# A due-time plan for the attention part of a fused attention, Fourier-mixing and MLP kernel

## The chip, the cores and the metric

The kernel runs on one core of a Trainium2 chip. Its five engines work in parallel, each through its own queue in the queue's order: TensorE (PE) with its matmuls and, beside them, weight loads; VectorE (DVE); ScalarE (ACT); GpSimd (POOL); and SyncE (SP), which here issues DMAs. An instruction that waits for a semaphore holds up everything behind it on its engine. The metric is the device time of one execution in microseconds (us).

## The reference

Batch 8, 8 heads, 576 positions, 64 values a head, all in f32. Causal attention with a decay bias comes first; then a Fourier mixing over positions and channels, a layer norm and an MLP. Cut to what matters:

```python
cum = np.cumsum(np.maximum(s, 0), axis=-1)
bias = -(cum[:, :, :, None] - cum[:, :, None, :])
scores = where(causal, -1e9, scale * q @ k.T + minimum(bias, 0))
attn = exp(scores - max); attn /= attn.sum() + 1e-9
x = (attn @ v).transpose(0, 2, 1, 3).reshape(8, 576, 512)
u = x + real(fft(fft(x, axis=1), axis=2))
un = (u - mean) / sqrt(var + 1e-6)
out = u + relu(un @ w1) @ w2            # 512 -> 2048 -> 512
```

## The kernel before

**Attention.** The 64 heads are handled as `NP` = 32 pairs, four pairs a batch. A pair `i` goes through the same steps, each a generator that yields between its instructions. `load` brings `qk` (SP's DMA). `high` has ACT round `qk` into `KQ`, and a DMA puts the rows of cumulated decay into it from `cumD`. `low` has two DMAs bring the rounded halves across partitions to `Q` and `K`, DVE form the remainder `K`, POOL the remainder `Q`, and a DMA load `va`. `maxes` has, for each head, five blocks of queries: PE multiplies into a PSUM bank `pm`, DVE takes the maximum of each query into a column of `Mx`; then PE transposes `Mx` into `pmt`, ACT copies that to `mt`, and a DMA puts `mt` as one row into `KQ`, so that the score product subtracts the maximum by itself. `scores` has PE multiply twice into a bank `ps`, ACT take the exponential `P`, POOL zero the causal corner. `av` has PE multiply `P` with `va` into `pav` (two banks a head), ACT copy the result to `stage` and `rows`, and DMAs collect the sums of the exponentials. `recip` has DVE take their reciprocals, and DMAs spread them through DRAM (`rd`) to `rb`. `finish` has POOL multiply, and for two of the four pairs of a batch DMAs bring the product, reversed, to `xs`.

**Mixing.** When a batch has its four pairs, `folds` adds and subtracts `xa` and `xs` (`Aw` on DVE, `Bw` on POOL, `Df`, `De`, `Do`), and `fourier` multiplies them with the tables in two stages (`pzs`, `pzc`, then `pyc`, `pys`) and stores `uD`.

**Conversion.** `convert_w` turns twelve pieces of the MLP's weights into two words each, beside the attention, and stores them in `wD`.

**What sets the order.** For pairs 0 to 30 a loop builds, for each pair, a list of these generators with quotas (of the next pair's `maxes`, this pair's `scores`, the last pair's `av`, a share of the mixing and so on), and `weave` takes from each in turn by its share. There only PE's order is the written one, by

```python
order.enter_context(tc.manual_schedule(engines={mybir.EngineType.PE}))
```

and a scheduler puts the instructions of the other engines in their queues. For the last pair, and all that comes behind it (the last mixing, the layer norm and the MLP), the order is written out for all engines by a planner, `Flow`: each step is a generator that yields (engine, cost, what it depends on, ring of buffers) before each instruction and has a due time; the planner keeps a time at which each engine is free, and of the steps that can start next on an engine it places the one with the earliest due time:

```python
t, s = min(ready, key=lambda x: (x[1][3][0] is not None, x[0]))
engine = s[3][0]
t, s = min(((u, v) for u, v in ready if v[3][0] == engine and u <= t + 0.05), key=lambda x: x[1][1])
```

A due time sets an order only; on the chip an instruction starts when the one before it on its engine is through and its semaphores are there.

**Banks.** PSUM has three banks `ps` for scores and mixing (`bank`), and five banks under one tag `m` for `pm`, `pmt` and `pav`. The buffers `KQ`, `Q`, `K` are there three times, `P` four times, `xa` and `xs` twice.

**Behind the attention** the MLP takes two token tiles in a plain way and then seven in `fast_tile`, with PE's products `b`, `h` and `acc`.

## Time and profile before

| | us |
|---|---|
| three runs | 1404.06, 1411.13, 1412.85 |
| their median | 1411.13 |
| the profiled execution | 1416.26 |
| its span in the profile | 1414.6 |
| PE busy in it | 1280.3 (91%) |
| DVE busy | 817.8 (58%) |
| ACT busy | 634.4 (45%) |
| POOL busy | 517.0 (37%) |

The mean clock granted to PE over the span is 0.962 of full speed. A busy time adds up all instructions of an engine, over stages in which different things set the pace, so a share alone does not say what bounds the kernel. In the page's digit rows the span is cut in 40 slices of 35.4 us; a digit is the busy share in tenths. In a row of a window table the numbers are the engines' busy times in one stretch of the span, then the granted clock. In a timeline or a group, `[4.62 <-DMA xs<-xr]` says that the engine stood 4.62 us ahead of the instruction, and what ended that. `SPq` and `ACTq` are issues of DMAs on the queues of SP and ACT.

### The profile page before, as it was taken

What the parts mean: (1) busy time and instruction counts of PE and PEld (TensorE: products, weight loads), DVE (VectorE), ACT (ScalarE), POOL (GpSimd) and SP (SyncE); (2) the same over time, 40 slices, a digit from 0 to 9 for tenths busy, and PEclk for the clock granted to TensorE, in tenths of its full rate; (3) what the DMA queues carried; (4) which work ended last, traced back from release to release, by engine and by line L of the source; (5) the groups of instructions that cost most, each with busy time, mean ns of one, the idle gap of its engine ahead of it and who ended that gap; (6) DMA issues with size and microseconds to landing.
All of it is one profiled execution on the core that took longest, in us unless ns stands there. A gap on an engine that the chain in (4) does not pass through costs nothing.

```text
span 1414.6 us, 21592 instructions
## 1 busy us (share of the span) xinstructions
PE 1280.3 (91%) x7582; PEld 1117.6 (79%) x7582; DVE 817.8 (58%) x1786; ACT 634.4 (45%) x1452; POOL 517.0 (37%) x499
## 2 busy tenths in 40 slices
PE   4887878977989888889999989999999999999998
PEld 3665766766777767779888878888888888888887
DVE  6567655765776765575964577544445453544423
ACT  4665645655766664633641333333333333333321
POOL 6444544654466554554673243110201111021100
PEclk9998988998999999999999999999999999999999
DMA  8656345555555563564764332534434344343433
GB/s 196 164 146 171 103 137 169 140 155 152 169 155 155 155 179 104 191 207 155 242 209 150 105 127 90 171 127 140 143 118 165 107 159 130 130 162 103 145 111 119
DMA packets 119687, 210.79 MB, mean 149 GB/s; under 512 B 15801, under 2 KB 37753, under 8 KB 119579
## 3 DMA queue, kind: packets, MB, share of 16 engines
q1 hardware_dynamic: 117579, 206.36, 47.6%
q0 software_dynamic: 1712, 2.53, 0.9%
q8 instruction: 60, 0.98, 0.3%
q10 hardware_dynamic: 288, 0.52, 0.1%
q14 instruction: 48, 0.39, 0.1%
HBM read 153.69 MB, written 31.72 MB: 131 GB/s over the span
## 4 chain that ended last, share of the span: by engine, by line
PE 50%; DVE 5%; POOL 3%; ACT 3%; issue 2%; DMA 2%; SPq 0%; POOLq 0%; ACTq 0%; DVEq 0%
PE b L342 19%; PE acc L254 7%; PE acc L253 7%; PE acc L255 7%; PE h L1432 3%; PE acc L1414 1%; PE acc L1413 1%; PE acc L1412 1%; POOL we L89 1%; PE pav L877 1%; PE pavB L685 1%; DVE we L83 1%; DVE we L80 1%; DMA raw<-in_wP_dram 1%; PE pz L1016 0%
## 5 line engine op out<-in xcount | busy, mean ns | idle before, releaser
L621 PE MATMUL pm<-KQ 128*128 128x256 f32 (+3 forms) x384 | 161.5, 439 | 46.8 <-DVE Mx L628 28.0
L657 ACT ACTIVATE P<-ps 128x256 f32<-128x256 f32 x372 | 142.5, 394 | 122.4 <-PE ps L654 118.7
L685 PE MATMUL pavB<-P,va 128*128 128x320 f32 x600 | 184.4, 401 | 1.3 <-ACT stage L689 1.2
L653 PE MATMUL ps<-KQ 128*128 128x256 f32 x372 | 151.3, 409 | 34.2 <-ACT P L657 15.7
L254 PE MATMUL acc<-zh,w2l 128*128 128x512 f32 x452 | 179.5, 397 | 0.0
L253 PE MATMUL acc<-zh,w2h 128*128 128x512 f32 x452 | 178.9, 396 | 0.0
L255 PE MATMUL acc<-zl,w2h 128*128 128x512 f32 x452 | 177.4, 393 | 0.0
L300 POOL TENSOR_TENSOR w<-w,o 128x512 f32<-128x512 f32 x28 | 38.2, 1373 | 346.6 <-DVE o L296 309.1
L628 DVE CUSTOM_DVE_ANT_0 trash<-pm,amask 128x128 bf16<-128x128 f32 (+3 forms) x256 | 123.6, 483 | 49.4 <-PE pm L621 34.3
L621 PEld LDWEIGHTS pm<-KQ 128*128 128x128 f32 x384 | 80.4, 212 | 70.2 <-DVE Mx L628 38.0
L653 PEld LDWEIGHTS ps<-KQ 128*128 128x128 f32 x372 | 76.2, 205 | 59.3 <-ACT P L657 22.0
L334 ACT ACTIVATE zh<-cs 128x256 fp32r<-128x256 f32 x112 | 58.8, 525 | 141.7 <-DVE cs L354 88.2
L654 PE MATMUL ps<-Q,K 128*128 128x256 f32 x372 | 119.2, 323 | 3.2 <-POOL Q L601 3.2
L601 POOL TENSOR_TENSOR Q<-qk,Q 64x576 fp32r<-64x576 f32 x64 | 100.4, 1584 | 44.2 <-DMA Q<-KQ 35.0
L598 DVE TENSOR_TENSOR K<-qk,KQ 64x576 fp32r<-64x576 f32 x64 | 61.4, 960 | 90.6 <-ACT KQ L584 82.3
L685 PEld LDWEIGHTS pavB<-P,va 128*128 128x128 f32 x600 | 105.3, 204 | 6.3 <-ACT stage L689 2.7
L335 DVE SCALAR_TENSOR_TENSOR zl<-cs,zh 128x256 fp32r<-128x256 f32 x112 | 65.4, 584 | 69.3 <-ACT zh L334 69.3
L342 PEld LDWEIGHTS b<-bh,wh 128*128 128x128 f32 x448 | 84.2, 189 | 24.8 <-DVE cs L354 5.4
L255 PEld LDWEIGHTS acc<-zl,w2h 128*128 128x128 f32 x452 | 85.1, 188 | 19.2
L660 POOL TENSOR_SCALAR_AFFINE_SELECT P<-P 128x512 f32<-128x512 f32 x62 | 44.2, 713 | 133.4 <-ACT P L657 130.8
L342 PE MATMUL b<-bh,wh 128*128 128x256 f32 x448 | 89.2, 281 | 4.1 <-DVE cs L354 4.1
L342 PE MATMUL b<-bh,wl 128*128 128x256 f32 x448 | 89.1, 280 | 0.0
(263 smaller groups left out, 3119.3 us busy)
## 6 DMA issues: line engine op xcount, KB each, us to landing
w2h<-w2D SPq DMA_DIRECT2D x128, 256.0 KB
w2l<-w2D SPq DMA_DIRECT2D x128, 256.0 KB
qk<-in_qkT_dram SPq DMA_DIRECT2D x32, 576.0 KB
raw<-in_wP_dram SPq DMA_DIRECT2D x32, 512.0 KB
va<-in_vA_dram SPq DMA_DIRECT2D x32, 480.0 KB
u<-uD SPq DMA_DIRECT2D x10, 1024.0 KB
Q<-KQ SPq DMA_DIRECT2D x32, 288.0 KB
K<-KQ SPq DMA_DIRECT2D x32, 288.0 KB
```

Of the source, the lines that this page charges most:

```text
L253: nc.tensor.matmul(acc[j], a[:, cs], y, start=first, stop=False)
L254: nc.tensor.matmul(acc[j], b[:, cs], y, start=False, stop=False)
L255: nc.tensor.matmul(acc[j], a[:, cs], z, start=False, stop=final)
L335: nc.vector.scalar_tensor_tensor(out=y[1][:, at], in0=src, scalar=0.0, in1=y[0][:, at].bitcast(F32), op0=ALU.max, op1=ALU.subtract)
L342: nc.tensor.matmul(p[:, 0:256], a[:, j * 128:(j + 1) * 128], b[:, j], start=start and i == 0, stop=i == 5, skip_group_check=not start)
L601: nc.gpsimd.tensor_sub(q1[64:128, h], qk[0:64, h], q1[0:64, h].bitcast(F32))
L621: nc.tensor.matmul(p[:, :n], qy[:, h, 128 * c:128 * c + 128], ky[:, h, k0:k0 + n], start=True, stop=True)
L628: nc.vector.tensor_tensor_reduce(out=trash[:, :n], in0=p[:, :n], in1=amask[:, m0:m0 + n], scale=1.0, scalar=first if x else NEG, op0=ALU.a ...
L653: nc.tensor.matmul(p[:nk, :n], ky[:, h, ksl], qy[:, h, a:a + n], start=True, stop=False)
L654: nc.tensor.matmul(p[:nk, :n], k1[:, h, ksl], q1[:, h, a:a + n], start=False, stop=True)
L657: nc.scalar.activation(P[:nk, o:o + a + n - lo], p[:nk, lo - a:n], AF.Exp, scale=0.125)
L685: nc.tensor.matmul(p[:, a - lo:n], va[:nk, c, vs], P[:nk, o:o + w], start=c == 0, stop=c == cs[-1])
```

## The change

The loop of quotas goes. All engines get the written order from the start, and everything ahead of the MLP (loading, maxima, scores, V products, reciprocals, folds, mixing, tables, conversion) becomes a set of generators of the one planner. Their due times come from a table `PR`, in us behind the start of their pair, with `T` = 16.03 us from pair to pair; the due times of what follows are set off by `O` = `T*L - 4.0`. The DMA of the row of maxima goes from SP's queue to ACT's. PSUM's five shared banks become three for `pm` and `pmt` and two for `pav`. The tables are loaded at due time `T*2`, on POOL's queue as before. Two memsets of `Mx` go. The computation, the tiles and the numbers of matmuls stay as they are. The core of the diff:

```diff
+PR = {'high': -1.41, 'hstep': 1.51, 'low': -1.81, 'lstep': 1.29, 'qs': -1.26, 'mx': 0.36, 'mxh': 2.95, 'mxc': 0.92, 'mt': 9.83, 'sc': -1.53, 'sch': 7.21, 'scs': 0.66, 'sel': 9.19, 'av': 8.0, 'avh': 10.43, 'avk': 5.44, 'rc': 2.01, 'fin': 10.5, 'fold': 4.51, 'fj': 1.4, 'fst': 1.02, 'fou': 7.13, 'gap': 5.72, 'fo2': 28.57, 'fo3': 33.4, 'gap2': 0.47, 'cv': -0.18, 'T': 16.03}
...
-order.enter_context(tc.manual_schedule(engines={mybir.EngineType.PE}))
-for i in range(NP - 1):
-    ...
-    weave(*streams)
-order.close()
 order.enter_context(tc.manual_schedule())
...
 def maxes(i):
...
-                    p = psm.tile([128, 512], F32, tag="m", name="pm", bufs=5)
+                e, hold = yield pe(mm(n), ev("rows", i), ev("k", i, h), ev("q", i, h), ring=(ring("psm", 3), 1))
+                p = psm.tile([128, 512], F32, tag="m", name="pm", bufs=3)
...
+        for h in range(2):
+            for c in range(5):
+                flow.add(one(h, c), T * (i - 1) + PR['mx'] + PR['mxh'] * h + PR['mxc'] * c)
+        e, hold = yield pe(0.1, ev("max", i), ring=(ring("psm", 3), 1))
...
         nc.scalar.copy(mt, p[0:10, 0:128])
-        nc.sync.dma_start(out=qy[2:3].bitcast(F32)...
+        hold.add(e)
+        e = yield ("ACT", 0.15, (), None)
+        nc.scalar.dma_start(out=qy[2:3].bitcast(F32)...
+        e = after(e, 2.6 + MARGIN)
...
-                p = psm.tile([128, 512], F32, tag="m", name="pav" + tg, bufs=5)
+                    p = psm.tile([128, 512], F32, tag="v", name="pav", bufs=2)
...
+    def pair(i):
+        yield from load(i) if i >= 3 else ()
+        flow.add(high(i), T * (i + PR['high']), PR['hstep'])
+        yield wait(ev("q", i, 1))
+        flow.add(low(i), T * (i + PR['low']), PR['lstep'])
+        flow.add(maxes(i), T * (i - 1) + PR['mt'])
+        yield wait(ev("row", i), ev("low", i), *(at(("scored", i - 1)) if i else ()))
+        flow.add(scores(i), T * i - 1.0)
+        yield wait(ev("va", i), ev("P4", i, 0))
+        flow.add(av(i), T * i + 7.0)
+        yield wait(ev("sums", i))
+        flow.add(recip(i), T * (i + 1) + PR['rc'])
+        yield wait(ev("rb", i), *(at(("out", i - 1)) if i else ()))
+        flow.add(finish(i), T * (i + 1) + PR['fin'])
...
+    def batches():
+        for b in range(NB):
+            yield wait(*(ev("out", 4 * b + j) for j in range(4)))
+            due = O + PR['fo2'] if b == B else T * (4 * b + PR['fold'])
+            flow.add(folds(b, due), due, 0.5 if b == B else PR['fst'])
+            yield wait(ev("folded", b))
+            due = O + PR['fo3'] if b == B else T * (4 * b + PR['fou'])
+            flow.add(fourier(b, due, PR['gap2'] if b == B else PR['gap']), due, 1.0 if b == B else PR['gap'])
...
+    flow.add(cum_rows(), 0.0)
+    flow.add(pairs(), -100.0)
+    flow.add(load_tables(), T * 2.0)
+    flow.add(batches(), 0.0)
+    for part in range(2):
+        flow.add(conversion(part), T * (PR['cv'] + part), T * (NP - 5) / (7 * NC))
+    flow.add(tail(), O)
```

How the rows of the engines' queues move is shown at three places. The first is DVE's queue about the fold of batch 3 (`Aw`, `Df`, `De`, `Do`), which before lies within the maxima of pair 19 (`Mx_137<-pm`). Before:

```order
L628 ISA Mx_137 128x1
L481 TENSOR_TENSOR ym<-yc,pys 128x290
L482 TENSOR_TENSOR yp<-yc,pys 128x290
L412 TENSOR_TENSOR Aw<-xa,xs 128x576
L628 ISA trash,Mx_137<-pm,amask 128x512
L628 ISA Mx_137 128x1
L624 TENSOR_REDUCE M_3398<-pm 128x1
L417 TENSOR_TENSOR Df<-Aw 128x289
L628 ISA trash,Mx_137<-pm,amask,M_3398 128x320
L628 ISA Mx_137 128x1
```

The same fold in DVE's queue of the change, behind the maxima of the same pair (there `Mx_151`):

```order
L574 ISA trash,Mx_151<-pm,amask 128x512
L574 ISA Mx_151 128x1
L569 TENSOR_REDUCE M_3575<-pm 128x1
L574 ISA trash,Mx_151<-pm,amask,M_3575 128x320
L574 ISA Mx_151 128x1
L708 TENSOR_SCALAR sums<-sums 32x36
L782 TENSOR_TENSOR Aw<-xa,xs 128x576
L790 TENSOR_TENSOR Df<-Bw 128x288
L710 RECIPROCAL sums<-sums 32x36
L795 TENSOR_TENSOR Do_3593<-Df,Do_3592 128x288
L802 TENSOR_TENSOR Df<-Aw 128x289
```

The fold came ahead of the last maxima of the pair; now it stands behind all of them, with the rest of the fold in one block of twenty rows ahead of the next pair's maxima.

The second place is PE's queue from the transposition `pmt` of pair 26 to that pair's own scores (before, `KQ_122`). Before:

```order
L633 MATMUL pmt<-ident,Mx_136 10x128
L653 MATMUL ps<-KQ_122 128x320
L654 MATMUL ps<-Q_125,K_128 128x320
L476 MATMUL pys<-ssin_84,zs_4574 128x290
L476 MATMUL pys<-ssin_85,zs_4574 128x290
L476 MATMUL pys<-ssin_84,zs_4575 128x290
L685 MATMUL pavB<-P,va 128x320
L653 MATMUL ps<-KQ_122 128x256
L654 MATMUL ps<-Q_125,K_128 128x256
```

In the change, where the pair's scores take `KQ_117`:

```order
L586 MATMUL pmt<-ident,Mx_150 10x128
L676 MATMUL pav<-P,va 128x320 x3
L676 MATMUL pav<-P,va 128x192
L676 MATMUL pav<-P,va 128x64
L615 MATMUL ps<-KQ_117 128x256
L616 MATMUL ps<-Q_120,K_123 128x256
L615 MATMUL ps<-KQ_117 128x320
L616 MATMUL ps<-Q_120,K_123 128x320
```

Where scores of the pair before, mixing and V products lay between transposition and first score, it is now the V products of one half head.

The third place is the DMA of the row of maxima of pair 28 (`KQ<-mt`). Before, in SP's queue:

```order
L111 DMA wD<-we 128x512
L694 DMA sums<-stage 16x1x36
L703 DMA rd<-sums 32x36
L428 DMA rows<-xs 1x16x36
L97 DMA raw<-in_wP_dram 128x1024
L706 DMA rb<-rd 64x576 x2
L636 DMA KQ_122<-mt 1x10x128
```

In the change, in ACT's queue:

```order
L621 ACTIVATE P<-ps 128x64
L689 COPY stage<-pav 128x320
L849 CAST zs_5298<-pz 96x256
L590 CAST mt<-pmt 10x128
L593 DMA KQ_116<-mt 1x10x128
L849 CAST zc_5296<-pz 96x258
L621 ACTIVATE P<-ps 128x256
```

The DMA leaves SP's queue, in which it stood behind others, and follows directly on the copy that makes its row.

## The prediction

> **What bounds the kernel now.** I read the page first: how busy TensorE (PE) is, slice by slice, and the clock it was granted.

> ```profile
> span 1414.6 us, 21592 instructions
> PE 1280.3 (91%) x7582; PEld 1117.6 (79%) x7582; DVE 817.8 (58%) x1786; ACT 634.4 (45%) x1452; POOL 517.0 (37%) x499
> PE   4887878977989888889999989999999999999998
> PEclk9998988998999999999999999999999999999999
> ```

> PE is the busiest engine, but its 91% is an average over two halves. In the first sixteen slices it reads 7 to 9 and the clock dips to 8; later both stand at 9. So I cut the span by stage. Attention reaches from the first score product of pair 0 (28.6) to that of pair 31 (568.9), 31 pair periods; all other cuts in it are also at a pair's first score product.

> ```profile
> core 0: us, PE busy (x) PEld busy (x) DVE busy (x) ACT busy (x) POOL busy (x), PEclk, DMA share, GB/s
> 28.60:568.90 540.30, 451.09 (x2434) 379.05 (x2434) 346.23 (x993) 329.25 (x806) 280.00 (x285) 0.92 0.55 151
> 97.10:568.90 471.80, 393.82 (x2146) 332.25 (x2146) 309.99 (x882) 283.26 (x697) 251.50 (x253) 0.92 0.53 149
> 568.90:803.30 234.40, 218.02 (x1355) 194.84 (x1356) 152.48 (x208) 100.02 (x190) 120.86 (x101) 0.96 0.55 183
> 803.30:1414.00 610.70, 600.22 (x3769) 537.08 (x3767) 296.75 (x525) 194.93 (x441) 96.26 (x80) 1.00 0.40 133
> 153.90:170.00 16.10, 14.42 (x91) 12.57 (x92) 10.62 (x32) 11.42 (x28) 8.85 (x8) 1.00 0.56 144
> 361.60:376.60 15.00, 12.92 (x73) 10.21 (x72) 9.39 (x28) 10.64 (x27) 8.41 (x11) 1.00 0.65 192
> 376.60:407.90 31.30, 28.54 (x181) 25.27 (x180) 19.57 (x67) 22.27 (x56) 15.82 (x17) 1.00 0.61 164
> 444.50:474.50 30.00, 29.03 (x181) 25.27 (x180) 18.84 (x65) 21.70 (x55) 14.71 (x16) 1.00 0.61 171
> 170.00:193.20 23.20, 17.30 (x90) 14.92 (x89) 8.96 (x32) 10.15 (x26) 5.73 (x8) 0.85 0.30 87
> 338.20:361.60 23.40, 16.97 (x88) 14.64 (x88) 16.88 (x43) 11.96 (x29) 14.47 (x14) 0.85 0.37 100
> 407.90:429.00 21.10, 18.14 (x97) 14.42 (x96) 18.70 (x41) 11.39 (x29) 15.10 (x15) 0.86 0.58 162
> 547.90:568.90 21.00, 16.97 (x83) 14.41 (x83) 13.90 (x39) 8.93 (x25) 11.16 (x12) 0.84 0.29 81
> ```

> This is the table to learn from. Behind 803 PE is busy 600.2 of 610.7 us at clock 1.00: nothing is left there. Attention has 89.2 us without PE work (540.3 - 451.1) and a clock of 0.92. It isn't evenly slow: the four rows at clock 1.00 hold one, one, two and two pairs, 92.4 us for six, **15.4 us a pair**. The four rows below them hold one pair each and take 22.2 us on average with about the same number of matmuls, and the clock in them is 0.84 to 0.86. A good pair and a bad pair do the same work; the bad one stands in a gap first and runs slowly after it.

> What ends PE's gaps in attention (total, times, longest):

> ```profile
> PE pm L621 <- DVE Mx L628: 26.3, 16, 6.0
> PE ps L653 <- ACT P L657: 15.7, 13, 5.3
> PE pmt L633 <- DVE Mx L628: 14.0, 11, 3.4
> PE ps L653 <- DMA KQ<-mt: 13.7, 9, 3.8
> ```

> The maxima on VectorE (DVE) lead, yet DVE is busy 346 of 540 us. One gap, of the bad pair at 338.2, shows why it is late all the same (the engines' own timelines):

> ```profile
> 341.86 0.45 DVE L482 TENSOR_TENSOR yp<-yc,pys 128x290 f32<-128x290 f32 x1
> 346.93 1.96 DVE L412 TENSOR_TENSOR Aw<-xa,xs 128x576 f32<-128x576 f32 x1 [4.62 <-DMA xs<-xr]
> 348.80 0.68 DVE L628 CUSTOM_DVE_ANT_0 trash<-pm,amask 128x512 bf16<-128x512 f32 x1
> 349.55 0.58 PE L621 MATMUL pm<-KQ 128*128 128x256 f32 x1 [6.02 <-DVE Mx L628]
> 350.23 0.44 ACT L67 CAST De<-Df 128x289 fp32r<-128x289 f32 x1 [7.75 <-DVE Df L417]
> ```

> DVE reached the first fold `Aw` of a batch and stood 4.62 us for the DMA that brings `xs`. The maxima were behind it in line, so PE stood 6.02; ScalarE (ACT) had its own fold copy next in line and stood 7.75. Nobody was overloaded: **an instruction was queued too early**. What the order decides is the bound here.

> **The change, part by part.** The instructions stay the same on every engine, but for 32 row DMAs that go from SP to ACT and two small memsets that go. So its price is in waits alone.

> *Order.* In the rows of the change the fold stands behind all maxima of its pair, and nothing of the next transposition hangs on it but the next pair's maxima. That takes away the kind of gap shown. The term: the 26 pairs from 97.1 to 568.9 took 471.8 us, 18.15 each; at the pace of the good pairs, 15.4, they would take 400.4, so **71.4 us is what order can give** at that pace. It holds the idle and the slow clock behind it (0.92 over 471.8 us is 38 us of clock, more than half of it). Why I take the good pace whole: good pairs hold Fourier matmuls too (91 matmul records in the row at 153.9, as in the bad rows), and DVE (about 10 us), ACT (11) and GpSimd (8) fit into 15.4 with room. Bounds: 0, and for the better side 14.5, the better half of the rows (15.0 alone, 30.0 for two), somewhat under which no row goes; that would be 23 us more.

> *Row of maxima.* The transposition `pmt`, ACT's copy `mt`, the DMA of the row, and the next pair's first score product are one chain.

> ```profile
> 506.01 0.27 PE L633 MATMUL pmt<-ident,Mx 128*10 128x128 f32 x1
> 506.65 0.24 ACT L635 CAST mt<-pmt 10x128 fp32r<-10x128 f32 x1
> 511.07 1.14 SPq L706 DMA_DIRECT2D rb<-rd  x2
> 512.34 0.84 SPq L636 DMA_DIRECT2D KQ<-mt  x1
> 512.34 2.47 DMA KQ<-mt
> 514.94 0.55 PE ps L653
> 570.27 2.78 PE pav L877 x14
> 1408.73 0.38 ACTq L303 DMA_DIRECT2D out_dram<-u  x1
> ```

> Here `mt` ended at 506.89 and its DMA was issued at 512.34, 5.45 us late: SP's queue had `rb<-rd` ahead of it, which waits itself. On ACT the DMA follows the copy. What the queue costs is in the 13.7 us above, and the good pairs are free of it, so the 15.4 holds this gain already and I don't count it again.

> But the change also lets PE arrive earlier. In the order before, some 3 us of matmuls stood between transposition and first score; in the commonest pattern of the change it is five products of V: 3 x 320 + 192 + 64 = 1216 columns. One head's V product has 1600 columns and took 2.78 us (the row at 570.27), so these are 2.1 us. The chain needs 0.64 to the copy's start, 0.24 for it and 2.60 from issue to the score (512.34 to 514.94): 3.5 us, or 3.1 with ACT free as soon as the transposition ends (0.27). PE waits 1.0 to 1.4 us a pair where it waited 0 in a good pair. I take 1.1, near the lower end, since a wait of PE lets DVE and ACT catch up: 26 x 1.1 = **28.6 us given back**. Bounds: 0 (all of it is caught up) and 36.

> [...]

> *ACT as issuer.* An issue on ACT's queue took 0.38 us (last row), 32 of them 12 us, beside 211 us in which ACT is idle in attention: 0 on the path. Were that cover gone, 12. Behind the issue stand copies of Fourier banks and the next exponentials; PE waits for those.

> *Banks.* Maxima get three, V products two of their own, where all shared five. A V product no longer waits for a maximum; a fourth maximum waits for the first. DVE, at 0.68 for the longest, sets that pace either way. 0; bounds: the 26.3 us row either way, gone or once more.

> *The rest.* Conversion and folds get due times, the tables load later on an idle GpSimd queue, and pairs 0 to 4 (540.3 - 471.8 = 68.5 us) and all behind 569 keep their time: 0. Behind 569 there are 16.4 us without PE work to win or lose.

> Sum: -71.4 + 28.6 = -42.8. The profiled execution took 1416.3 (span 1414.6 and 1.7 around it), so 1373.5; on the median of 1411.1 that is **1368 us**.

> **The rivals.**

> *Faster: the row is hidden as well.* PE's short waits are caught up, and clock 1.00 holds throughout: -71.4, 1340 us. For it: at 376.6 and 444.5 four pairs in a row ran at clock 1.00 with 1 us idle each. Against: the chain of 3.1 us is longer than 2.1 us of cover. [...]

> *No change: fold pairs stay long.* In the rows at 338.2 and 407.9, both with folds, DVE works 16.9 and 18.7 us, more than 15.4, and the change puts one block of twenty such rows between two pairs' maxima. If seven fold pairs stay at 22.2, they keep 7 x 6.8 = 48 us: -42.8 + 48 = +5, 1416. Against: the neighbours need 10 us of DVE, so over four pairs it averages under 12, and PE has other work to do meanwhile.

> *The change doesn't do what it says.* Due times only order; engines still start by semaphores. If transfers land at other times than assumed, half of the blocked starts come back elsewhere: -35.7 + 28.6 = -7, 1404.

> *Slower: ACT becomes the gate of the row.* With all engines in a fixed order, `mt` stands behind exponentials, which wait for PE. Its worst case before:

> ```profile
> 418.08 0.27 PE L633 MATMUL pmt<-ident,Mx 128*10 128x128 f32 x1
> 422.68 0.24 ACT L635 CAST mt<-pmt 10x128 fp32r<-10x128 f32 x1
> ```

> 4.6 us from transposition to copy, 4.3 over the best. It decides from 26 x (1.0 + x) = 71.4, x = 1.75 us of mean lateness. At half of the worst, 2.2, it is 26 x 3.2 = 83: +12, and gaps over 3 us bring the slow clock, 3.3 us each (0.15 of 22.2) in perhaps every second pair, 43: some 1465, without the clock 1423. Against: 0.64 in the pair above, and the order shown has the DMA right behind the copy.

> **How the numbers follow.** Forecast 0.57; faster rival 0.20; fold pairs 0.08; order that doesn't hold 0.07; ACT as gate 0.08. A measurement here tells about 1% from no change, 1397 to 1425. The forecast and the faster rival lie below, with a small part of the forecast above 1397 (28.6 at its upper bound and a pace of 16 instead of 15.4): faster 0.77; same: that part, the fold rival and the third, 0.15; slower 0.08. The range reaches to the faster rival's 1340 less a little for a better pace, 1335, and up past 1404, to 1410.

> **What the next profile should show.** Right: the pairs' period near 16.5 us with few over 19; the clock of attention at 0.97 or more; hardly any wait of `pm` and `pmt` for DVE, no gap over 4 us behind `Aw`; waits of the first score product for the row in most pairs, about 1 us each, 30 in all. Wrong: fold pairs over 20 us with DVE full; `mt` more than 1.75 us behind `pmt` on average; the clock still at 0.92; or a changed time behind the attention.

## The result

The changed kernel takes **1450.9 us** (median of four runs, 1443.7 to 1453.6) against 1410.4 beside it: ratio 1.029, 95% interval 1.0235 to 1.0337. It is slower by 2.9%; I had forecast 1368, faster by 3%, with a range up to 1410.

The page of the changed kernel, the same lines as of before:

```profile
span 1447.5 us, 21561 instructions
PE 1286.0 (89%) x7582; PEld 1136.7 (79%) x7582; DVE 819.7 (57%) x1784; ACT 631.4 (44%) x1452; POOL 514.7 (36%) x499
PE   3876878788888787889988989999999999999998
PEclk9988889999999888999999999999999999999999
```

No engine got much more to do (PE 1286.0 us for 1280.3); PE's digits in the first half are still mostly 7 and 8, and its clock now reads 8 in seven slices, where it did in four. The stages, cut at the same places of the program (all of attention; pairs 5 to 30; the two stages behind it):

```profile
core 0: us, PE busy (x) PEld busy (x) DVE busy (x) ACT busy (x) POOL busy (x), PEclk, DMA share, GB/s
32.25:595.48 563.23, 458.01 (x2447) 399.36 (x2448) 344.13 (x996) 325.76 (x803) 271.15 (x284) 0.90 0.52 143
112.83:595.48 482.65, 393.48 (x2138) 346.71 (x2139) 298.47 (x863) 278.15 (x687) 237.13 (x247) 0.90 0.50 139
595.48:836.00 240.52, 219.49 (x1354) 195.96 (x1355) 159.51 (x218) 99.86 (x192) 127.65 (x100) 0.96 0.53 174
836.00:1447.00 611.00, 600.11 (x3766) 536.90 (x3765) 299.89 (x525) 194.96 (x441) 95.48 (x80) 1.00 0.41 133
```

The 26 pairs that I had forecast at 429 us (400.4 and 28.6) took 482.7; before they took 471.8. The first score product comes 3.7 us later, pairs 0 to 4 take 80.6 us for 68.5, and the stage behind attention 240.5 for 234.4: 22 us more which I had put at nothing. What PE waits for in the changed kernel (total, times, longest), over the whole span:

```profile
PE ps L615 <- DMA KQ<-mt: 93.7, 27, 10.6
PE pm L564 <- ACT KQ L513: 12.3, 2, 11.1
PE pm L564 <- DVE Mx L574: 7.2, 12, 1.3
```

The order did what was forecast of it: waits of `pm` for DVE's maxima fell from 28.0 to 7.2 us, and none is over 1.3. But one wait has taken the place of all others: the first score product of nearly every pair stands for the row of maxima, 93.7 us in all, 76.0 of them in the 26 pairs, where I had put 28.6. One such pair, on PE, ACT and SP:

```profile
416.64 0.27 PE L586 MATMUL pmt<-ident,Mx 128*10 128x128 f32 x1
416.99 2.27 PE L676 MATMUL pav<-P,va 128*128 128x320 f32 x10
423.60 0.58 PE L615 MATMUL ps<-KQ 128*128 128x256 f32 x1 [4.35 <-DMA KQ<-mt]
417.23 0.24 ACT L590 CAST mt<-pmt 10x128 fp32r<-10x128 f32 x1
417.50 0.76 ACTq L593 DMA_DIRECT2D KQ<-mt  x1
414.91 0.67 SPq L523 DMA_DIRECT2D Q<-KQ  x1
415.63 0.59 SPq L445 DMA_DIRECT2D qk<-in_qkT_dram  x1
416.34 0.91 SPq L544 DMA_DIRECT2D va<-in_vA_dram  x1
418.39 1.05 SPq L525 DMA_DIRECT2D K<-KQ  x1
```

ACT is prompt: 0.6 us from transposition to copy, and the DMA goes out at once. The row then takes 6.1 us from issue to score, while SP's large transfers (288 to 576 KB each) are under way. PE has 2.3 us of V products for it, and stands 4.35.

### The profile page after: what moved, and what is told of

It is laid out like the page before. It is cut to its first block, busy times and chain, and to the rows that moved or that the text cites. A ratio compares the mean times of both kernels' runs of the same rounds, so it can differ in the third digit from the quotient of the medians.

```text
span 1447.5 us, 21561 instructions
## 1 busy us (share of the span) xinstructions
PE 1286.0 (89%) x7582; PEld 1136.7 (79%) x7582; DVE 819.7 (57%) x1784; ACT 631.4 (44%) x1452; POOL 514.7 (36%) x499
## 4 chain that ended last, share of the span: by engine, by line
PE 56%; DVE 6%; DMA 5%; POOL 3%; issue 2%; ACT 2%; SPq 0%; POOLq 0%; ACTq 0%; DVEq 0%
PE b L343 18%; PE acc L255 7%; PE acc L254 7%; PE acc L256 7%; DMA KQ<-mt 3%; PE pav L676 3%; PE h L1316 3%; PE ps L615 2%; PE pm L564 2%; PE ps L616 2%; PE pz L843 1%; PE acc L1296 1%; PE acc L1297 1%; PE acc L1298 1%; PE py L879 1%
## 5 line engine op out<-in xcount | busy, mean ns | idle before, releaser
L615 PE MATMUL ps<-KQ 128*128 128x256 f32 (+2 forms) x384 | 139.1, 371 | 98.6 <-DMA KQ<-mt 93.7
L676 PE MATMUL pav<-P,va 128*128 128x320 f32 (+4 forms) x896 | 213.4, 377 | 6.8 <-POOL Q L532 3.4
L621 ACT ACTIVATE P<-ps 128x320 f32<-128x320 f32 (+4 forms) x384 | 137.7, 393 | 134.4 <-PE ps L616 129.6
L676 PEld LDWEIGHTS pav<-P,va 128*128 128x128 f32 x896 | 164.6, 201 | 40.2 <-issue 6.7
L615 PEld LDWEIGHTS ps<-KQ 128*128 128x128 f32 x384 | 86.4, 225 | 108.0 <-DMA KQ<-mt 65.3
L564 PE MATMUL pm<-KQ 128*128 128x256 f32 (+3 forms) x384 | 123.6, 384 | 21.7 <-ACT KQ L513 12.3
L616 PE MATMUL ps<-Q,K 128*128 128x256 f32 (+2 forms) x384 | 130.0, 346 | 0.1
L564 PEld LDWEIGHTS pm<-KQ 128*128 128x128 f32 x384 | 76.9, 217 | 35.9 <-DVE Mx L574 14.5
L532 POOL TENSOR_TENSOR Q<-qk,Q 64x576 fp32r<-64x576 f32 x64 | 94.2, 1488 | 18.2 <-DMA Q<-KQ 11.5
L343 PE MATMUL b<-bh,wh 128*128 128x256 f32 x448 | 89.2, 281 | 4.0 <-DVE cs L355 4.0
L343 PE MATMUL b<-bh,wl 128*128 128x256 f32 x448 | 89.2, 281 | 0.0
L616 PEld LDWEIGHTS ps<-Q,K 128*128 128x128 f32 x384 | 86.9, 226 | 2.7 <-POOL Q L532 0.3
```

The source lines that it names most:

```text
L343: nc.tensor.matmul(p[:, 0:256], a[:, j * 128:(j + 1) * 128], b[:, j], start=start and i == 0, stop=i == 5, skip_group_check=not start)
L532: nc.gpsimd.tensor_sub(q1[64:128, h], qk[0:64, h], q1[0:64, h].bitcast(F32))
L564: nc.tensor.matmul(p[:, :n], qy[:, h, 128 * c:128 * c + 128], ky[:, h, k0:k0 + n], start=True, stop=True)
L615: nc.tensor.matmul(p[:, :n], ky[:, h, ksl], qy[:, h, a:a + n], start=True, stop=False)
L616: nc.tensor.matmul(p[:, :n], k1[:, h, ksl], q1[:, h, a:a + n], start=False, stop=True)
L621: nc.scalar.activation(P[:, o:o + a + n - lo], p[:, lo - a:n], AF.Exp, scale=0.125)
```

## The experiments

Four things could be the cause: the **flight** of the row (it now leaves while SP goes on issuing), the **cover** (how much PE has to do between transposition and first score), the **clock** behind the waits, or the new **order** itself. The table gives the steps of that chain, as means over pairs 5 to 30 worked out from the timelines of each run, in us. The two middle steps end at the start of the first score product; "PE work between" is the time from the start of `pmt` to it less the wait just ahead of it, so the 0.27 us of the transposition itself are in it:

```
run            pmt to mt   issue to first score   pmt to first score   PE work between   PE waits
before              1.08                   3.56                 5.38              4.98       0.39
after               0.65                   4.18                 5.12              2.20       2.92
after_sp            0.62                   3.48                 4.41              2.22       2.19
refit_only          0.56                   5.99                 6.83              6.13       0.70
plan_know           0.77                   6.74                 7.78              7.75       0.04
```

Where PE waits (after, after_sp), "pmt to first score" is the length of the chain; where it doesn't, it is what PE had to do.

**Who issues the row** (after_sp): SP in place of ACT, at the same place of the plan.

```diff
-        nc.scalar.dma_start(out=qy[2:3]...
+        nc.sync.dma_start(out=qy[2:3]...
```

> The changed kernel, with the DMA of the row of maxima issued by SP at the same place of the plan; no other engine's order moves. Theory A (contention): on ACT's queue the row meets the bulk transfers that SP goes on issuing; from issue to first score it took 4.2 us on average (before: SP's own queue was still at that time, and the row's last packet was through 2.0 us after the issue). Then with SP it falls to about 2.7, PE's wait for the row from 2.9 us a pair to about 1.4: 47 us less, with some clock 50 to 60, so 1390 to 1405. Theory B (only the cover between transposition and first score counts, 2.2 us against 5.0): no matter who issues, 1440 to 1460. Third: the row stands in SP's line behind other waits, and all behind it comes late: over 1460.

Measured: 1416.5, ratio to before 1.006 [1.003, 1.009], 34 us less than the change. From issue to score it fell from 4.18 to 3.48, the wait from 2.92 to 2.19. That fits contention, but it is a part: the gain is less than I expected, and the wait that stays is twice the one I had forecast. The 34 us also hold what ACT no longer has to issue, so they aren't the price of the flight alone.

**No late row** (after_early): the decay, which is there early, is subtracted in place of the maximum.

```diff
-        nc.sync.dma_start(out=cumD[2, 1], in_=zero)
+        nc.sync.dma_start(out=cumD[2, 1], in_=cumhl[:R, 0:S].bitcast(F32))
...
+                nc.sync.dma_start(out=qy[2:3, h, 0:S].bitcast(F32), in_=cumhl[r0 + h:r0 + h + 1, 0:S].bitcast(F32))
...
-        nc.scalar.dma_start(out=qy[2:3]..., in_=mt...)
```

> The changed kernel without the row's late DMA: the row that is subtracted is the cumulated decay itself, which comes with the earlier rows of the pair (the softmax is the same for any row), while the maxima, their transposition and copy are still made, so all work but 32 small DMAs stays. If the row is all that keeps the new order from its gain: PE's 94 us of waits for it go, and clock with them (0.90 to 0.97 or so in attention), 1310 to 1345. If other waits take their place (maxima on DVE, P on ACT): 1370 to 1410. If the order itself is bad: over 1410.

Measured: **1345.2**, ratio 0.954 [0.951, 0.957]; the stage of the 26 pairs:

```profile
97.79:491.57 393.78, 364.38 (x2142) 316.57 (x2140) 305.21 (x863) 272.65 (x686) 239.53 (x245) 0.97 0.62 169
```

15.15 us a pair, where I had taken 15.4 from the good pairs. The order is right, and the late row with its DMA loses its gain.

**The row in the old order** (before_early): the same edit in the kernel before.

> The kernel before with the decay in place of the row of maxima, as in the run of the change without the late DMA: tells what the row costs in the old order. By its trace 14 us of PE's waits and some lateness on SP: 1385 to 1403, so the new order is worth 45 to 60 us where neither has the row. If the old order gains as much as the new one (over 60): 1345 or less.

Measured: 1401.5, ratio 0.995 [0.992, 0.997]. With the other three it makes a square:

| | old order | new order |
|---|---|---|
| with the late row | 1410 | 1451 |
| without it | 1401 | 1345 |

The row costs 9 us in the old order and 106 in the new one; the new order is worth 56 where the row isn't in its way. The two don't add: the old order was slow in other places, and its 5 us of other matmuls hid most of the row. The edit takes the issue of the DMA away too, in the new order from ACT, so the 106 hold that as well.

**The queue in the old order** (before_act): the DMA of the row on ACT, in the kernel before.

> The kernel before with only the queue of the row's DMA changed, SP to ACT. Theory A (contention): the row lands 1 to 1.6 us later; the 5.0 us of matmuls between transposition and first score hide most of it: PE's waits for the row from 14 us to 25 to 40, 1410 to 1435. Theory B: the 12 us of lateness in SP's line go, nothing else: 1395 to 1410.

Measured: 1409.4, ratio 1.001 [0.999, 1.003]. In the old order, with its 5 us of cover, it doesn't matter who issues.

**The clock** (after_fill): spare matmuls in the wait.

```diff
+                for _ in range(16 if i and not (h or c or a) else 0):
+                    nc.tensor.matmul(p[:, :n], k1[:, h, ksl], q1[:, h, a:a + n], start=True, stop=True)
                 nc.tensor.matmul(p[:, :n], ky[:, h, ksl], qy[:, h, a:a + n], start=True, stop=False)
```

> The changed kernel with 16 spare matmuls of 256 columns (about 1.8 us) on the bank of the first score product of each pair, ahead of that product and overwritten by it; they need the low words but not the row, so they fill a part of the wait. If the clock behind the gaps is a main part of the loss: granted clock of attention from 0.90 to 0.95 or more, 1415 to 1435. If it is idle time alone: 1445 to 1465, as the matmuls cost time where the row is already there.

Measured: 1428.7, ratio 1.014 [1.011, 1.018]. The 26 pairs:

```profile
112.27:572.90 460.63, 418.88 (x2555) 373.39 (x2555) 302.01 (x862) 276.79 (x687) 235.73 (x246) 0.96 0.53 144
```

PE does 416 matmuls more for nothing there and the stage is 22 us shorter, with the clock at 0.96 for 0.90. So the clock behind the waits is a part of the loss.

**The banks** (after_banks): `pm`, `pmt` and `pav` from five shared banks, the written order as in the change.

> The changed kernel with its written order, but pm, pmt and pav from five shared banks as before, in place of three and two. If the split costs nothing: 1440 to 1460. If maxima need the five banks: 1430 or less. If V products then wait for maxima: 1465 or more.

Measured: 1448.4, ratio 1.029 [1.023, 1.035]. What the split costs or brings is too small to tell from the change's 1450.9.

**Why the cover is so short.** The change's planner has a step that waits for the row, but without an engine: it puts no time on the steps behind it. The score product's own step names only its bank, so the planner places it as soon as PE is free, 2.1 us of planned work behind the transposition on average, as if the row were there. Telling it (of the low words too) is one line:

```diff
-                e, hold = yield pe(2 * mm(n), ring=(ring("ps", 3), 1))
+                e, hold = yield pe(2 * mm(n), ev("row", i), ev("low", i), ring=(ring("ps", 3), 1))
```

Three kernels take it apart: with the table `PR` of the change (know_old), with a table fitted anew to the plan that knows (plan_know), and with that table alone (refit_only).

> The same with the table of the change as it was: only the planner's knowledge of the wait is added, 6.3 us of cover on average, but the maxima come no earlier, so that PE has to stand elsewhere. If cover is all, 1350 to 1380. If the due times must move with it: waits of the maxima for free KQ buffers and for DVE take the place of the row's, 1390 to 1430.

> The changed kernel with the planner told of the wait (the score product's step depends on the row and the low words, which in the change only a step without an engine waited for, so that the products were placed 2.1 us of work behind the transposition), and the table PR fitted anew to that plan: 6.7 us of matmuls then stand between transposition and first score on average, 4.6 at least. ACT issues the row as in the change. Theory cover: the chain of 5.1 us is hidden in most pairs, PE's wait for the row falls from 94 us to about 20, 1350 to 1385. Theory contention: the row's flight of up to 6.8 us goes beyond any such cover, 1385 to 1410. If the table fits the plan and not the chip: over 1410.

> The changed kernel with the new table of the run that was told of the wait (1380), but the planner not told of it. The table alone brings 5.5 us of cover on average, but six pairs have under 2 us. If the table does it all: 1375 to 1385. If the pairs without cover pay their 3 to 5 us with clock: 1390 to 1420. If knowing is all: over 1430.

Measured: know_old **1411.0**, ratio 1.002 [0.999, 1.005]; plan_know **1380.1**, 0.979 [0.974, 0.984]; refit_only **1384.6**, 0.984 [0.980, 0.987]. In plan_know the wait for the row is all but gone:

```profile
PE ps L615 <- ACT P L621: 22.2, 19, 7.7
PE pm L564 <- DVE Mx L574: 15.8, 19, 7.4
PE ps L615 <- DMA KQ<-mt: 5.5, 4, 4.2
```

In know_old it is 11.3 us, but PE stands 45.2 us for the maxima, since they are due no earlier. So knowing alone gains 40 us on the change, the table alone 66, both together 71: the maxima have to come earlier, which the table does, and whether knowing then adds anything is open (4.5 us, with intervals that overlap). With cover most of the row's 106 us are won back while ACT still issues it, so most of the loss goes with the lack of cover. The new table moves all other due times too; what that brings by itself I did not separate.

**The queue again, under cover** (plan_know_sp): plan_know's written order, the row issued by SP.

> The kernel with cover (1380), its written order kept, the row issued by SP. Where the chain is hidden, the queue shouldn't matter, as in the kernel before (1409 and 1409): 1372 to 1388. If contention still costs there: 1365 or less. If SP's line makes rows and what stands behind them late: over 1390.

Measured: **1367.2**, ratio 0.971 [0.966, 0.975], 13 us under plan_know and below what I expected. The row was hidden in both, so this isn't the flight; PE's waits for ACT's exponentials fell from 22.2 to 14.2:

```profile
PE ps L615 <- ACT P L621: 14.2, 10, 6.4
PE ps L615 <- DMA KQ<-mt: 7.1, 1, 7.1
```

It fits 32 issues of 0.73 us (their median in the change) which ACT no longer has ahead of its exponentials; by which way it reaches PE I did not separate.

**Further versions.** A further fit of the table (plan_know2), and a kernel that leaves the maxima out altogether with the decay subtracted in their place (no_max2).

> The planner told of the wait, as in the run before with that and a new table, and the table fitted further: the plan ends 3.6 us earlier, with 5.6 us of matmuls of cover on average and 4.0 at least. 1365 to 1380 if the plan's gain holds on the chip; if gains of a few us in the plan don't reach the chip, 1375 to 1395.

> The decay in place of the row of maxima, and now the maxima, their matmuls, transposition and copy left out too, with five banks for V products and a table fitted to that (softmax of the reference, as any row may be subtracted, but without the guard against large products of q and k). Against the run with idle maxima (1345) the plan is 43 us shorter: 1290 to 1320. If attention is then bound by ACT's exponentials and copies or by DMA: 1320 to 1340.

Measured: 1374.9, ratio 0.976 [0.972, 0.980], 5 us under plan_know where the plan had 3.6, but with intervals that overlap, so this gain isn't clear of the noise; and **1306.2**, 0.928 [0.925, 0.932]. The last is the fastest by far, and any row may be subtracted in a softmax; but it has no guard against large products of q and k, which the reference and both kernels have. Of the kernels with the maximum, plan_know_sp is the fastest.

## Why the prediction was wrong

**The order: right.** I took 15.4 us a pair from the good pairs, -71.4 us for 26. The run without the late row has 15.15, 78 us less than before. Some of that is what the row cost in the old order: against before_early, where the 26 pairs took 456.9 us, the new order is worth 63. The reading that carried it (good and bad pairs do the same work, so the good pace can be had throughout) holds.

**The row of maxima: the step that failed.** I put the chain at 3.1 to 3.5 us, the cover at 2.1, and the wait at 1.1, with 36 us as the upper bound. The cover was about right (2.2, the transposition included), though not that of the old order, where I had some 3 us and it was 5.0. The chain is 5.1 us: from issue to score it took 4.18, where I had taken 2.60 from a single row at 512.34. That is the term that was mis-sized, by 1.6 us a pair. The 2.60 came from a quiet moment: SP's queue, held up by `rb<-rd`, had issued nothing from 509.02 to 511.07. In the pair of the change shown above SP had issued three large transfers (`Q`, `qk`, `va`) in the 2.6 us ahead of the row. The rows of the change by what the DMA engines did meanwhile, two quiet and two busy ones, from issue to score:

```profile
173.05:175.09 2.04, 2.03 (x11) 1.23 (x9) 1.82 (x5) 1.22 (x3) 0.00 (x0) 1.00 0.03 5
457.74:459.89 2.15, 0.00 (x0) 0.03 (x1) 0.87 (x5) 0.00 (x0) 0.00 (x0) 1.00 0.27 71
417.50:423.60 6.10, 1.75 (x9) 1.28 (x7) 3.08 (x4) 0.43 (x1) 5.66 (x5) 0.81 0.89 241
491.72:498.56 6.84, 1.66 (x10) 1.20 (x8) 0.37 (x1) 0.43 (x1) 5.16 (x5) 0.84 0.77 231
```

At a DMA share of 0.03 and 0.27 the row took 2.0 and 2.2 us, at 0.77 and 0.89 over 6. Over the 26 pairs: six with a share under 0.4 took 2.6 us on average, six between 0.4 and 0.75 took 3.9, fourteen above took 5.0. In after_sp the same three classes hold 7, 9 and 10 rows, with 2.2, 3.0 and 4.8 us: the flight goes with the share, whoever issues.

The row's own ten packets of 512 bytes, in the traces, leave out what PE had to do meanwhile: over the 26 pairs the last of them was through 1.8 us after the issue before, 3.1 in the change and 2.7 in after_sp, but only 2.0 in before_act, where ACT issues in the old order. So most of the longer flight came with the moment at which the new order sends the row, less with the queue; the DMA share up to that packet was 0.28 before, 0.37 in before_act, 0.74 in the change. No run changed the other transfers alone, so that they are what holds the row up is argued from this.

The profile of before had this to see, at its start; in pairs 5 to 30 no such window had a share over 0.64. Two windows of it, each from the row's issue to the first score, the first at pair 1, the second the one that I priced by:

```profile
33.29:39.06 5.77, 2.65 (x11) 1.87 (x11) 0.30 (x2) 1.75 (x5) 4.05 (x7) 0.87 1.18 284
512.34:514.95 2.61, 0.01 (x1) 0.04 (x1) 1.77 (x5) 1.61 (x4) 1.17 (x1) 0.50 0.36 132
```

The forecast let the flight stay as it was in that one row. With ACT issuing it was 2.0 to 6.8 us from issue to score, by what else was under way.

**The clock: left out.** The sum put no clock behind its waits of 1.1 us. They were 2.9 us on average, and what comes with waits of that length stood in the profile of before. Of the four bad rows two, at 170.0 and 338.2, have a gap of 5.3 and 6.0 us. The two others, at 407.9 and 547.9, read 0.86 and 0.84 as well, and these are the longest waits of PE in them:

```profile
422.83 0.39 PE L653 MATMUL ps<-KQ 128*128 128x256 f32 x1 [2.31 <-ACT P L657]
556.57 0.58 PE L621 MATMUL pm<-KQ 128*128 128x256 f32 x1 [2.53 <-DVE Mx L628]
```

The clock was at half from 423.25 to 430.08 and from 556.38 to 559.79. So the slower rival's "gaps over 3 us" was not the whole of it: before, each of the seven such gaps in pairs 5 to 30 (3.3 to 6.0 us) came with half clock, but so did these two. In the change, one pair's scores behind the wait of 4.35 us:

```profile
423.60:427.00 3.40, 3.40 (x12) 3.21 (x13) 0.82 (x3) 1.37 (x4) 0.00 (x0) 0.50 0.32 95
```

PE is busy throughout at half clock. With and without the late row the 26 pairs hold the same matmuls (2138 and 2142 records), and PE is busy 393.5 against 364.4 us. So of the row's 88.9 us there (482.7 - 393.8), **29.1 are slower matmuls, with the clock at 0.90 for 0.97, and 59.8 idle time**. The forecast had 28.6 for both.

**ACT as issuer: 0, bound 12.** Right in the old order (1409 and 1408). In the new one the move back to SP was worth 34 us, and 13 where the row was hidden. The bound was 32 times 0.38 us, from the issue of an output store; an issue of the row on ACT took 0.73 us (median), 23 us for 32. **Banks: 0**, right. **The rest: 0**, wrong by 22 us: 12.1 in pairs 0 to 4, 3.7 ahead of them, and 6.1 behind attention. Of these the run without the late row keeps 7.2 in pairs 0 to 4 (75.7) and 5.0 behind attention (239.4), so these aren't the row's; which part of the change brings them stays open. **The rivals:** the slower one gave 1423 to 1465 and had the arithmetic of a late row, but the wrong cause: `mt` is 0.65 us behind `pmt`, the lateness is in the DMA. The rivals on fold pairs and on due times that don't hold were both wrong: PE's waits for the maxima are small, and without the late row the order has its pace. Of the signs of being wrong that I named, two showed: a clock of attention not over 0.92 (0.90), and a changed time behind the attention.

## What to carry to other kernels

A wait that cost nothing may have been hidden by the very disorder that is to be removed (here the row cost 9 us in the old order and 106 in the new one): when an order is tightened, price each DMA on the path by the cover that will be left, and by its flight among the transfers that will then be under way (here 4.18 us on average), not by a flight from a quiet moment (2.60). Look whether a planner's wait puts time on the step that really waits. And a short wait in every period can cost PE twice: here, in 26 pairs, 59.8 us idle and 29.1 of slower matmuls.

## What the hardware showed

At pair 0 record and pace differ. Behind PE's waits of over 10 us there (10.58 in the change, 10.50 without the late row) the record reads full clock, but the matmuls ran as at half. In the change a score product of 448 columns took 0.58 us at 33.38 and 0.37 at 36.73; in the half-clock stretch from 421.23 to 428.06 one took 0.58, and behind it 0.37. Without the late row it was 0.57 at 33.94 and 0.37 at 37.58. The sums above leave this time out.
